# One change to a Fourier filter, expert layer and gated layer kernel: the first batch's transform rebuilt, and the weights converted at other places

## The chip, the cores and the metric

The kernel runs on one core of a Trainium2 chip. The metric is the device time of one execution, in microseconds (us); below, the median of three runs of the kernel before stands beside the one execution that was profiled.

## The reference

Three layers in a row, all in float32. `x` has 8 batches of 3072 positions of 256 features.

```python
X = np.fft.rfft(x, axis=1)                 # attn: a filter in the frequency domain
y = np.fft.irfft(X * (filt_r + 1j * filt_i)[None], n=3072, axis=1)
x1 = np.maximum(np.maximum(y @ w1, y @ w2), y @ w3) @ w_out      # 256 -> 768 -> 256
x_prev = shift_by_one_position(x1)         # zeros for the first position
xk, xr = mu_k * x1 + (1 - mu_k) * x_prev, mu_r * x1 + (1 - mu_r) * x_prev
k = np.maximum(xk @ w_k, 0)                # 256 -> 1024
out = sigmoid(xr @ w_r) * (k * k @ w_v)    # 1024 -> 256
```

[...]

## The kernel before, in words

A batch's transform of length 3072 is split into a transform of length 256 over one index (a matmul), a multiplication with twiddle factors, a transform of length 12 over the other index, the filter, and the same way back. Batches 1 to 7 do the transform of length 12 with VectorE's additions (`fft_all`, spread in small steps over the matmuls of the layers by a meter that counts costs; the order that comes out is fixed when the program is built). The first batch has nothing to hide behind, so `fft0` does it with matmuls and a trip through scratch memory in DRAM, ahead of everything else:

1. **Stage 1**, six units u. `load_x` brings a quarter of a unit of `x` in each of four transfers (`fetch_x`). `split_x` makes `xH` (VectorE cast) and `xL` (GpSimd subtraction). `stage1` is 12 matmuls into the PSUM tiles `re` and `im`. `twiddle` makes products `t` on ScalarE and sums `at` on VectorE, and writes `at` to the scratch `a0` in four transfers, two issued by SyncE (SP) and two by ScalarE (ACT). `clear_pad` zeroes rows 32 to 63 of nine tiles on ScalarE, since the two halves of the rows sit at partitions 0 and 64.
2. **The chunk loop**, eight chunks c of 1024 columns, two iterations each. `load_a` reads a chunk of the scratch into `rt`, `load_f` the filter into `ft` (four transfers), `spread_f` copies `ft` to its second half on ScalarE. An iteration is a matmul to `x0`, two VectorE products `zr` and `zi` with the filter, two matmuls back to `pv` (two iterations later), a ScalarE copy to `vo`, and per chunk two transfers of `vo` to the scratch `v0`. Chunk 0 alone needs extra matrices and extra filter rows (`special_f`, and a few bytes more behind `spread_f`).
3. Between these iterations, the generator `w1gen` converts w1, w2 and w3, 12 parts of 384 columns in two steps each. `W_STEPS` says how many steps go after each piece of `fft0`; in the loop it is two.

Then `load_v` brings the first tile back from `v0`, `untwiddle` and `stage_b` end the inverse transform, w_out is converted (`load_wo`), and the tiles t of the first layer begin: 48 tiles, each six `fblock`s (18 matmuls, two VectorE maxima `hm`, a split to `hH` and `hL`) and one `x1_out`. Between the first tiles' matmuls stand the first units of batch 1's transform (`load_x`, `fold` to `xe`, `dft_rows`).

Each engine runs its own instructions strictly in the order of the program, waits included. A transfer is issued by an engine's queue in the same order. SP issues nearly all of them.

Of the kernel before, what the change touches and what calls it, by code (L numbers as in the profile page):

```python
# [38 lines left out]
def own_tables():  # L39
# [35 lines left out]
    def spread(blocks, off, rows):  # L75
        n = 2 * M2
        o = np.zeros((off + n * len(blocks), 3, off + n * len(blocks)))
        for e, mats in enumerate(blocks):
            for i, m in enumerate(mats):
                for a in range(2):  # L80
                    for b in range(2):
                        part = m[a * M2:(a + 1) * M2, b * M2:(b + 1) * M2]
                        part = np.kron(part, np.eye(NH)) if rows else np.kron(np.eye(NH), part)
                        o[off * a + n * e:off * a + n * e + n, i, off * b + n * e:off * b + n * e + n] = part
        return o

    here, first = (fwd, inv, turned), (fwd0, inv0, turned0)
    named = {"m12": spread((here, here), 64, True), "m12s": spread((first, here), 64, True), "mside": spread((first,), 32, False)}
    named |= {"dft": rows(m), "up": rows(m + P), "idft": idft, "tw": tw}
# [3 lines left out]
def tile_fourier_moe_rwkv(ctx, tc, xl, fl, f0, dft24m, dft, idft, tw, w1, w2, w3, wo, muk, mur, wk, wv, wr, out):  # L93
# [5 lines left out]
    R1 = 4 * M2  # L99
    R2 = 64 + R1  # L100
# [3 lines left out]
    a0 = dram.tile([2, 2, RS, KC, P], F32, name="a0", tag="a0")  # L104
    v0 = dram.tile([2, 2, RS, KC, P], F32, name="v0", tag="v0")
# [75 lines left out]
    def from_f64(pool, tags, hi, lo, st, n):  # L181
        def tmp(dt, k):
            tag, bufs = tags[k]
            return pool.tile([P, n], dt, tag=tag, bufs=bufs, name=f"wt{k}")
# [8 lines left out]
        v, sg, r = tmp(I32, 1), tmp(I32, 2), tmp(I32, 1)  # L193
        u1, u2 = tmp(F32, 1), tmp(I32, 2)
# [6 lines left out]
        rf = tmp(F32, 2)  # L201
        scaled(rf, r, 2.0 ** -35)
        yield
        hb, pw = tmp(I32, 3), tmp(I32, 2)
# [61 lines left out]
    def fetch_x(xt, b, u):  # L266
        lower = xl[b // 2, :, :, u, b % 2].rearrange("h n (o x) -> o n h x", o=2)
        upper = xr[b // 2][:, 2 * u + b % 2].rearrange("h n (o x) -> o n h x", o=2)
        for k in range(2):
            for odd in range(2):  # L270
                if k == 0:
                    rows = lower[odd, :64]
                elif b:
                    rows = upper[1 - odd]
                else:
                    rows = lower[odd, 64:]
# [43 lines left out]
    def fft_all():  # L320
# [40 lines left out]
        load_f(0)  # L361
# [9 lines left out]
        for b in range(1, B):  # L371
            A = fp.tile([P, NH, M2, 2, P], F32, tag="A", name="A")
            for u in range(NU):
# [3 lines left out]
                if b == 1 and u < NH:  # L377
                    mirror_x(1, u)
                yield STOP
# [51 lines left out]
    AB = 4  # L431
    FBUF = 3
    LAG = 2
    ZB = 3
    mat_sb = pp.tile([R2, 3, R2], F32, name="mat_sb")
    mats_sb = pp.tile([R2, 3, R2], F32, name="mats_sb")
    upH = pp.tile([P, 2, P], F32R, name="upH")
    upL = pp.tile([P, 2, P], F32R, name="upL")

    def fft0():  # L440
        xt_t, xs_t, ps_t = {}, {}, {}

        rts = [m1.tile([R2, CH0], F32, tag=tag, name="rt", bufs=bufs) for tag, bufs in (("vt", 2), ("vt", 2), ("xo", 1))]
        fts = [pp.tile([R2, 2, CH0], F32, tag=f"f{i}", name="ft") for i in range(FBUF)]
        pads = [t[32:64] for t in rts] + [t[32:64, k] for t in fts for k in range(2)]

        def clear_pad():
            if pads:
                nc.scalar.mul(out=pads.pop(0), in_=tw_sb[32:64, 0, 0:1].to_broadcast([32, CH0]), mul=0.0)

        def load_x(u):
            xt_t[u] = pp.tile([P, 2, 512], F32, tag="a", name="xt", bufs=AB)
            fetch_x(xt_t[u], 0, u)

        def split_x(u):
            xt = xt_t.pop(u)
            xH = pp.tile([P, 2, 512], F32R, tag="b", name="xH", bufs=2)
            xL = pp.tile([P, 2, 512], F32R, tag="c", name="xL", bufs=2)
# [5 lines left out]
        def stage1(u):  # L464
            xH, xL = xs_t.pop(u)
            ps_t[u] = [bank([P, NH, 2, P], name) for name in ("re", "im")]
            for k, o in enumerate(ps_t[u]):
                of = o.rearrange("p h q c -> p (h q c)")
                mm3(of, dftH[:, k], dftL[:, k], xH[:, 0], xL[:, 0], True, False)
                mm3(of, upH[:, k], upL[:, k], xH[:, 1], xL[:, 1], False, True)  # L470

        def twiddle(u):
# [21 lines left out]
        rows_f = f0.rearrange("(k e h) r (kh x) -> e kh k h r x", e=2, h=NH, kh=2)  # L494

        def fetch_f(c):
            cs = slice(c * CH0, (c + 1) * CH0)
            for kh in range(2):
                for h in range(NH):
                    nc.sync.dma_start(out=fts[c % FBUF][RS * kh + h:RS * (kh + 1):NH], in_=rows_f[0, kh, :, h, :, cs])  # L500


        def special_f(t, at):
            for h in range(NH):
                nc.sync.dma_start(out=at(t, h), in_=rows_f[1, 0, 0:6, h, :, 0:P])

        def load_f(c):
            fetch_f(c)
            if c == 0:
                special_f(fts[0], lambda t, h: t[12 + h:24:NH, :, 0:P])  # L510

        def spread_f(c, k):
            nc.scalar.copy(out=fts[c % FBUF][64:R2, k], in_=fts[c % FBUF][0:R1, k])
            if c == 0:
                nc.sync.dma_start(out=fts[0][64:66, k, 0:P], in_=rows_f[0, 0, 6, :, k, 0:P])

        def load_a(c):
            for r in range(2):
                nc.sync.dma_start(out=rts[c % 3][64 * r:64 * r + R1], in_=af[r * R1:(r + 1) * R1, c * CH0:(c + 1) * CH0])

# [572 lines left out]
```

## Time and profile before

| | |
|---|---|
| median of 3 runs | 3218.6 us (3214.14 to 3220.53) |
| the profiled execution | 3208.55 us, its span on the core 3206.8 us |
| TensorE (PE) busy in the span | 3085.1 us (96%) |
| VectorE (DVE) | 2142.3 us (67%) |
| ScalarE (ACT) | 1474.6 us (46%) |
| GpSimd (POOL) | 1340.1 us (42%) |
| mean granted TensorE clock | 0.986 |

PE is busy almost throughout; only the first twentieth of the span shows it much below that. Times in rows are counted from the start of the span.

### The profile page before, as it was taken

Reading aid. Unit: us, or ns where it says so; the run is one execution under the profiler, and the core shown is the slowest. Engines: PE = TensorE matmul, PEld = TensorE weight load, DVE = VectorE, ACT = ScalarE, POOL = GpSimd, SP = SyncE. Lnnn points to the kernel's source line nnn. Section 1 sums busy time; section 2 is a strip of 40 time slices with the busy share of each in tenths; the row PEclk is TensorE's granted clock in tenths of the full one; section 3 lists DMA queues with packets and bytes.
Section 4 is the critical chain, followed back from the end, with each engine's and each line's share of the span. In section 5 each row is a group of like instructions: output and inputs, shape, how many; then the busy total and the mean of one; then the engine's idle time right before and its main releaser. Section 6 shows DMA issues by size and latency. Waiting matters only on the chain. (4 is left out here: it accounts for less than half of the span.)

```text
span 3206.8 us, 43665 instructions
## 1 busy us (share of the span) xinstructions
PE 3085.1 (96%) x16596; PEld 2629.2 (82%) x16596; DVE 2142.3 (67%) x2825; ACT 1474.6 (46%) x2744; POOL 1340.1 (42%) x988
## 2 busy tenths in 40 slices
PE   4689999999999999999999999999999999999999
PEld 2368787888888888887888888988899988898998
DVE  3749879589498597796794733555655555565555
ACT  3643343433433433434333534555555555555554
POOL 2273453633634634535333433444444344444343
PEclk7989999999999999999999999999999999999999
DMA  5632212212322112122111211111111111111110
GB/s 149 189 114 66 86 66 106 86 47 76 107 88 80 53 66 93 41 84 88 47 47 47 86 34 43 53 53 56 54 50 50 53 50 54 59 50 50 50 53 34
DMA packets 110743, 221.37 MB, mean 69 GB/s; under 512 B 11477, under 2 KB 51773, under 8 KB 108733
## 3 DMA queue, kind: packets, MB, share of 16 engines
q1 hardware_dynamic: 106244, 213.86, 20.0%
q10 hardware_dynamic: 4288, 4.72, 0.6%
q8 instruction: 130, 2.13, 0.3%
q14 instruction: 81, 0.66, 0.1%
HBM read 139.55 MB, written 90.00 MB: 72 GB/s over the span
## 5 line engine op out<-in xcount | busy, mean ns | idle before, releaser
L127 POOL TENSOR_TENSOR hL<-hm,hH 128x512 fp32r<-128x512 f32 x288 | 435.2, 1511 | 864.3 <-ACT hH L739 862.5
L127 DVE TENSOR_TENSOR hm<-p,hm 128x512 f32<-128x512 f32 x576 | 394.8, 686 | 345.5 <-PE p L124 290.1
L124 PE MATMUL pv<-wvh,kl 128*128 128x256 f32 x1536 | 431.0, 281 | 8.2 <-POOL kl L127 5.8
L127 POOL TENSOR_TENSOR ml<-tm,mh 128x512 fp32r<-128x512 f32 x192 | 249.2, 1298 | 451.7 <-ACT mh L828 451.7
L122 PE MATMUL pv<-wvh,kh 128*128 128x256 f32 x1536 | 426.3, 278 | 0.0
L123 PE MATMUL pv<-wvl,kh 128*128 128x256 f32 x1536 | 426.1, 277 | 0.0
L127 POOL TENSOR_TENSOR kl<-sq,kh 128x512 fp32r<-128x512 f32 x192 | 248.9, 1296 | 267.7 <-ACT kh L852 121.4
L731 ACT COPY hm<-p 128x512 f32<-128x512 f32 x288 | 168.4, 586 | 415.2 <-PE p L124 409.9
L828 ACT CAST mh<-tm 128x512 fp32r<-128x512 f32 x192 | 119.2, 621 | 490.7 <-DVE tm L130 490.7
L123 PE MATMUL pk<-ml,wkh 128*128 128x512 f32 x768 | 304.9, 397 | 0.2 <-POOL ml L127 0.2
L124 PEld LDWEIGHTS pv<-wvh,kl 128*128 128x128 f32 x1536 | 288.3, 188 | 18.0 <-POOL kl L127 18.0
L122 PE MATMUL pk<-mh,wkh 128*128 128x512 f32 x768 | 299.8, 390 | 0.0
L124 PE MATMUL pk<-mh,wkl 128*128 128x512 f32 x768 | 299.4, 390 | 0.0
L122 PEld LDWEIGHTS pv<-wvh,kh 128*128 128x128 f32 x1536 | 290.1, 189 | 0.0
L130 DVE SCALAR_TENSOR_TENSOR sq<-pk,rl 128x512 f32<-128x512 f32 x384 | 249.8, 680 | 57.9 <-ACT rl L847 57.9
L123 PEld LDWEIGHTS pv<-wvl,kh 128*128 128x128 f32 x1536 | 288.3, 188 | 0.0
L130 DVE SCALAR_TENSOR_TENSOR tm<-xt,mu_sb,tm 128x512 f32<-128x512 f32 x192 | 194.4, 1013 | 131.6 <-ACT tm L139 131.6
L739 ACT CAST hH<-hm 128x512 fp32r<-128x512 f32 x288 | 179.5, 623 | 221.1 <-DVE hm L127 220.7
L127 DVE TENSOR_TENSOR ot<-pv,sg 128x512 f32<-128x512 f32 x96 | 66.4, 692 | 298.0 <-issue 222.5
L127 DVE TENSOR_TENSOR kl<-sq,kh 128x512 fp32r<-128x512 f32 x192 | 221.6, 1154 | 31.9 <-ACT kh L852 15.7
L852 ACT ACTIVATE kh<-rl 128x512 fp32r<-128x512 f32 x384 | 240.8, 641 | 0.0
L847 ACT ACTIVATE rl<-pk 128x512 f32<-128x512 f32 x384 | 226.8, 603 | 4.4 <-DMA x1s<-xo 2.3
(163 smaller groups left out, 8073.0 us busy)
## 6 DMA issues: line engine op xcount, KB each, us to landing
xt<-x1s SPq DMA_DIRECT2D x40, 768.0 KB
x1s<-xo SPq DMA_DIRECT2D x96, 256.0 KB
out_dram<-ot SPq DMA_DIRECT2D x96, 256.0 KB
F<-in_fl_dram SPq DMA_DIRECT2D x14, 1536.0 KB
vs<-T SPq DMA_DIRECT2D x14, 1536.0 KB
vt<-vs SPq DMA_DIRECT2D x42, 512.0 KB
xt<-in_xl_dram SPq DMA_DIRECT2D x108, 128.0 KB
xt<-xr SPq DMA_DIRECT2D x84, 128.0 KB
```

The costliest lines, as they stand in the source:

```text
L122: nc.tensor.matmul(o, lh, rh, start=first, stop=False)
L123: nc.tensor.matmul(o, lh, rl, start=False, stop=False)
L124: nc.tensor.matmul(o, ll, rh, start=False, stop=last)
L127: (eng or nc.vector).tensor_tensor(out=o, in0=a, in1=b, op=op)
L130: nc.vector.scalar_tensor_tensor(out=o, in0=a, scalar=s, in1=b, op0=op0, op1=op1)
L731: nc.scalar.copy(out=hm, in_=ps[0])
L739: nc.scalar.copy(out=hH, in_=hm)
L828: nc.scalar.copy(out=hi, in_=tf)
L847: nc.scalar.activation(out=rl, in_=ps, func=AF.Relu)
L852: nc.scalar.activation(out=kh, in_=rl, func=AF.Square)
```

## The change

`x` comes in six transfers of 512 KB, one per unit, all in flight from the start (six buffers), with even and odd positions side by side. The matrices of stage 1 come as one table (`dft0`). The scratch `a0` and `v0` is laid out so that a chunk's rows are contiguous: `rt` and `vo` have 96 rows without a hole, one transfer instead of two; `at` is written by two transfers per unit, both on SP. Only the six halves of the `ft` tiles are still cleared, one in each unit. The chunks run in the order 1, 2, 3, 0, 4 to 7, and the filter of the first two chunks is loaded within stage 1. The small filter rows of chunk 0 are issued by ScalarE, the side filter `fs_sb` in the second tile, batch 1's filter later. Of the conversions, 8 parts stay in `fft0` (four steps between stage 1 and the loop, then one per iteration); the second halves of w2 and w3 and all of w_out (8 parts of 384 columns) move into the first tile (`load_late`, three steps after each fblock).

```diff
+        def load_x(u):
+            xt_t[u] = pp.tile([P, NH, 2, 256], F32, tag="a", name="xt", bufs=NU)
+            nc.sync.dma_start(out=xt_t[u].rearrange("p h o x -> p h (o x)"), in_=xl[0, :, :, u, 0].rearrange("h n x -> n h x"))
...
-            rows = a0.rearrange("r kh s k c -> kh k r s c")
+            rows = a0.rearrange("r s kh k c -> r (kh k) s c")
             for ri in range(2):
-                for kh in range(2):
-                    (nc.sync if kh else nc.scalar).dma_start(
-                        out=rows[kh, :, ri, 4 * u:4 * u + 4],
-                        in_=at[KC * kh:KC * (kh + 1), ri].rearrange("p q h c -> p (q h) c"))
+                nc.sync.dma_start(out=rows[ri, :, 4 * u:4 * u + 4], in_=at[:, ri].rearrange("p q h c -> p (q h) c"))
...
+        order = [1, 2, 3, 0] + list(range(4, NC))
...
         for u in range(NU):
-            if u == 4:
...
             stage1(u)
-            if u + AB - 1 < NU:
-                load_x(u + AB - 1)
-            for _ in range(2):
-                clear_pad()
-            if u == 3:
-                load_f(0)
             if u + 1 < NU:
                 split_x(u + 1)
+            nc.scalar.mul(out=pads[u], in_=tw_sb[32:64, 0, 0:1].to_broadcast([32, CH0]), mul=0.0)
             if u:
                 twiddle(u - 1)
+            if u in (1, 3):
+                load_f(order[u // 2])
             yield
...
+    def load_late():
...
+        parts = [(w_sb[("w2", "w3")[i // 2]], i % 2, st[:, i]) for i in range(4)]
+        parts = [(h[:, k, 384:], l[:, k, 384:], p) for (h, l), k, p in parts]
+        parts += [(hf[:, c:c + 384], lf[:, c:c + 384], so[:, c:c + 384]) for c in range(0, FB1 * D, 384)]
+        before = None
+        for i, (hi, lo, src) in enumerate(parts):
+            gen = from_f64(None, None, hi, lo, src, 384, lt[:, i % 2])
+            next(gen)
+            yield
+            if before:
+                next(before, None)
+                yield
+            before = gen
+        next(before, None)
...
-        W_STEPS = [0] * 5 + [1, 0] + [2] * 40
+        W_STEPS = [0] * NU + [4] + [1] * 40
...
         load_v(0)
-        wogen = load_wo()
-        next(wogen)
+        lategen = load_late()
+        next(lategen)
+        load_v(1)
+        fftgen = fft_all()
+        next(fftgen)
...
             for f in range(FB1):
                 fblock(t, f, step)
+                if t == 0:
+                    run_later()
+                    for _ in range(3):
+                        next(lategen, None)
```

On ScalarE in stage 1, the order before, from the products of unit 0 (t out of `im` and `re`) on; the rows named DMA are the writes of `at` to the scratch that ScalarE itself issues:

```order
L139 ACTIVATE t_210<-im,tw_sb 128x256 [waits PE_49]
L139 ACTIVATE t_211<-re,tw_sb 128x256
L139 ACTIVATE t_214<-im,tw_sb 128x256
L139 ACTIVATE t_215<-re,tw_sb 128x256
L490 DMA a_57<-at 64x4x128 [waits DMAHW7_49,DVE_49]
L490 DMA a_57<-at 64x4x128 [waits DMAHW1_49,DVE_49]
L449 ACTIVATE ft<-tw_sb 32x1024 x2
L139 ACTIVATE t_254<-im,tw_sb 128x256 [waits PE_49,Activation_49]
```

The same place of the change:

```order
L152 ACTIVATE t_205<-im,tw_sb 128x256 [waits PE_49]
L152 ACTIVATE t_206<-re,tw_sb 128x256
L152 ACTIVATE t_209<-im,tw_sb 128x256
L152 ACTIVATE t_210<-re,tw_sb 128x256
L556 ACTIVATE ft<-tw_sb 32x1024
L152 ACTIVATE t_245<-im,tw_sb 128x256 [waits DVE_49,PE_49]
```

The two writes, which wait for VectorE, have left ScalarE's order, and one zeroing stands between the units instead of two.

On SP around the end of stage 1 before, with the side filter, the last writes of `at`, three weight loads, the reads of the scratch and the filter loads of the second chunk:

```order
L505 DMA fs_sb<-in_f_dram 6x2x128 [waits DMAHW2_49]
L490 DMA a_57<-at 64x4x128 [waits DMAHW3_49,DVE_49]
L490 DMA a_57<-at 64x4x128 [waits DVE_49]
L490 DMA a_57<-at 64x4x128 [waits DMAHW5_49,DVE_49]
L490 DMA a_57<-at 64x4x128 [waits DMAHW6_49,DVE_49]
L178 DMA wst<-in_moe_w_dram 128x768
L178 DMA wst<-in_moe_w_dram 128x768 [waits DMAHW0_49]
L178 DMA wst<-in_moe_w_dram 128x768 [waits DMAHW1_49]
L490 DMA a_57<-at 64x4x128 [waits DMAHW2_49,DVE_49]
L490 DMA a_57<-at 64x4x128 [waits DMAHW3_49,DVE_49]
L519 DMA rt<-a_57 48x1024 [waits DMAHW5_49,DMAHW4_49,DMAHW2_49]
L519 DMA rt<-a_57 48x1024 [waits DMAHW6_49,DMAHW3_49]
```

The same place of the change:

```order
L521 DMA ft<-in_f_dram 12x2x1024 [waits DMAHW1_49]
L509 DMA a_57<-at 128x4x128 [waits DMAHW2_49,DVE_49]
L509 DMA a_57<-at 128x4x128 [waits DMAHW3_49,DVE_49]
L509 DMA a_57<-at 128x4x128 [waits DMAHW4_49,DVE_49]
L509 DMA a_57<-at 128x4x128 [waits DMAHW5_49,DVE_49]
L509 DMA a_57<-at 128x4x128 [waits DMAHW6_49,DVE_49]
L509 DMA a_57<-at 128x4x128 [waits DMAHW7_49,DVE_49]
L191 DMA wst<-in_moe_w_dram 128x768 [waits DMAHW0_49]
L191 DMA wst<-in_moe_w_dram 128x768 [waits DMAHW1_49,DVE_49]
L191 DMA wst<-in_moe_w_dram 128x768 [waits DMAHW2_49,DVE_49]
L540 DMA rt<-a_57 96x1024 [waits DMAHW6_49,DMAHW5_49,DMAHW7_49,DMAHW4_49,DMAHW3_49]
```

The side filter's loads are gone from this place, the first chunks' filter is ahead of the last writes instead of behind the reads of the scratch, and three weight loads, two of which wait for VectorE, stand between the last write and the first read.

On VectorE in the first tile of the change, from the last of `stage_b` through the first two fblocks (`hm` are an fblock's maxima, `lt` a late conversion):

```order
L140 TENSOR_TENSOR yL<-y_824,yH 128x512
L140 TENSOR_TENSOR hm<-p_856,hm 128x512
L140 TENSOR_TENSOR hm<-p_857,hm 128x512
L205 TENSOR_SCALAR lt<-wlst 128x384
L203 TENSOR_SCALAR lt<-wlst 128x384
L205 TENSOR_SCALAR lt<-wlst 128x384
L143 SCALAR_TENSOR_TENSOR lt<-wlst,lt 128x384
L205 TENSOR_SCALAR lt<-wlst 128x384
L203 TENSOR_SCALAR lt<-wlst 128x384
L205 TENSOR_SCALAR lt<-wlst 128x384
L143 SCALAR_TENSOR_TENSOR lt<-wlst,lt 128x384
```

Before, the three conversions of w_out (18 operations of 512 columns) stood at this place as one block ahead of the first `hm`; now eight parts stand in pieces behind each fblock's two maxima.

## Rows read from the trace of the kernel before

**Rows 1.** The profile's page, part 1: busy time, share, instructions

```profile
PE 3085.1 (96%) x16596; PEld 2629.2 (82%) x16596; DVE 2142.3 (67%) x2825; ACT 1474.6 (46%) x2744; POOL 1340.1 (42%) x988
```

**Rows 2.** Windows by stage: stretch, length, busy time of each engine, clock, DMA share, GB/s

```profile
0.00:46.04 46.04, 24.56 (x72) 16.05 (x72) 17.38 (x38) 20.46 (x36) 16.36 (x20) 0.86 0.55 143
46.04:72.31 26.27, 4.42 (x8) 1.98 (x8) 0.00 (x1) 3.75 (x5) 0.00 (x0) 0.56 0.68 162
72.31:133.46 61.15, 44.05 (x94) 16.49 (x94) 55.21 (x105) 46.95 (x77) 12.20 (x12) 0.96 0.61 168
133.46:149.74 16.28, 5.72 (x24) 5.15 (x25) 1.89 (x5) 3.52 (x7) 2.54 (x2) 0.58 0.71 203
149.74:213.34 63.60, 50.96 (x198) 38.73 (x197) 31.24 (x54) 31.96 (x61) 39.71 (x32) 0.87 0.50 161
213.34:3206.80 2993.46, 2955.41 (x16204) 2550.85 (x16202) 2036.61 (x2624) 1367.96 (x2558) 1269.29 (x923) 1.00 0.18 62
```

**Rows 3.** Timeline, one unit of stage 1: start, duration, engine, line, operation

```profile
25.34 1.54 ACTq L490 DMA_DIRECT2D a<-at  x2
...
26.11 2.62 POOL L127 TENSOR_TENSOR xL<-xt,xH 128x512 fp32r<-128x512 f32 x2 [3.51 <-DVE xH L460]
...
26.93 2.00 ACT L449 ACTIVATE ft<-tw_sb 32x1024 f32<-32x1024 f32 x2 [2.92 <-DVE xH L460]
...
30.56 0.48 DVE L130 SCALAR_TENSOR_TENSOR at<-re,tw_sb,t 128x256 f32<-128x256 f32 x1 [4.19 <-ACT t L139]
...
31.86 1.26 ACTq L490 DMA_DIRECT2D a<-at  x2
```

**Rows 4.** Timeline, first matmul of stage 1's units 0, 1 and 2

```profile
6.18 0.77 PE L122 MATMUL re<-xH,dftH 128*128 128x512 f32 x1 [6.18 <-DVE xH L460]
...
12.65 0.48 PE L122 MATMUL re<-xH,dftH 128*128 128x512 f32 x1
...
15.53 0.39 PE L122 MATMUL re<-xH,dftH 128*128 128x512 f32 x1
```

**Rows 5.** Timeline, from the last write of the scratch to the loop's first product

```profile
55.20 1.28 SPq L490 DMA_DIRECT2D a<-at  x2
60.16 2.67 SPq L519 DMA_DIRECT2D rt<-a  x6
62.88 6.79 SPq L500 DMA_DIRECT2D ft<-in_f_dram  x8
...
64.20 0.74 PE L586 MATMUL x<-rt,mats_sb 112*112 112x128 f32 x2 [25.08 <-DMA rt<-a]
...
72.31 0.69 DVE L127 TENSOR_TENSOR zr<-x,ft 112x512 f32<-112x512 f32 x1 [26.27 <-DMA ft<-in_f_dram]
```

**Rows 6.** Windows, a stretch of stage 1 with the transfers near their limit

```profile
27.00:30.00 3.00, 2.18 (x8) 1.52 (x9) 0.00 (x0) 2.97 (x5) 1.73 (x2) 1.00 0.99 261
```

**Rows 7.** Timeline, one iteration of the chunk loop on VectorE and one on ScalarE

```profile
94.29 0.68 DVE L127 TENSOR_TENSOR zr<-x,ft 112x512 f32<-112x512 f32 x1
...
98.64 0.68 DVE L127 TENSOR_TENSOR zr<-x,ft 112x512 f32<-112x512 f32 x1
...
96.33 1.04 ACT L513 COPY ft<-ft 48x1024 f32<-48x1024 f32 x1 [0.86 <-ACT vo L567]
97.40 0.51 ACT L206 CAST w2h<-wt 128x384 fp32r<-128x384 f32 x1
...
99.40 0.57 ACT L567 COPY vo<-pv 112x512 f32<-112x512 f32 x1
99.99 1.05 ACT L513 COPY ft<-ft 48x1024 f32<-48x1024 f32 x1
```

**Rows 8.** Timeline, SP reads the first tile back; and batch 1's first matmul

```profile
136.16 2.63 SPq L673 DMA_DIRECT2D vt<-v  x4
...
168.99 0.79 PE L122 MATMUL re<-xH,dftH 128*128 128x512 f32 x1 [4.50 <-ACT xH L339]
```

**Rows 9.** Windows, the stretch in which batch 1's transform runs on VectorE

```profile
230.00:377.00 147.00, 142.74 (x656) 118.33 (x656) 143.28 (x174) 49.27 (x94) 58.35 (x36) 0.98 0.18 62
```

More of the change, by code (lines that the diff above doesn't have):

```diff
@@ L440, in fft0 @@
     def fft0():
         xt_t, xs_t, ps_t = {}, {}, {}
-        rts = [m1.tile([R2, CH0], F32, tag=tag, name="rt", bufs=bufs) for tag, bufs in (("vt", 2), ("vt", 2), ("xo", 1))]
+        rts = [m1.tile([RT, CH0], F32, tag=tag, name="rt", bufs=bufs) for tag, bufs in (("vt", 2), ("vt", 2), ("xo", 1))]
         fts = [pp.tile([R2, 2, CH0], F32, tag=f"f{i}", name="ft") for i in range(FBUF)]
[L445 to L449, printed above, removed]
@@ L496, in fetch_f, with load_f @@
-        def fetch_f(c):
+                nc.sync.dma_start(out=rows[ri, :, 4 * u:4 * u + 4], in_=at[:, ri].rearrange("p q h c -> p (q h) c"))
+        def load_f(c):
             cs = slice(c * CH0, (c + 1) * CH0)
             for kh in range(2):
+                first = kh == 0 and c == 0
                 for h in range(NH):
[L500 to L505, printed above, removed]
@@ L512, in spread_f @@
         def spread_f(c, k):
-            nc.scalar.copy(out=fts[c % FBUF][64:R2, k], in_=fts[c % FBUF][0:R1, k])
+            nc.scalar.copy(out=ft_t[c][64:R2, k], in_=ft_t[c][0:R1, k])
             if c == 0:
[L515 to L519, printed above, removed]
+                nc.scalar.dma_start(out=ft_t[0][64:66, k, 0:P], in_=rows_f[0, 0, 6, :, k, 0:P])
@@ L531, in fft0, with load_a, pieces @@
+        af = a0.rearrange("r s kh k c -> (r s kh) (k c)")
+        vf = v0.rearrange("r s kh k c -> (r s kh) (k c)")
+        z_t, vo_t = {}, {}
+        def load_a(c):
+            nc.sync.dma_start(out=rt_t[c], in_=af[:, c * CH0:(c + 1) * CH0])
+        def pieces(c, j):
+            return ((1, slice(0, P)), (0, slice(P, 512))) if c == 0 and j == 0 else ((0, slice(0, 512)),)
+        for u in range(NU):
             load_x(u)
+            if u == 2:
+                yield
         yield
+        pads = [t[32:64, k] for t in fts for k in range(2)]
@@ L583, in fft0 @@
+        for i in range(3):
+            load_a(order[i])
+        load_f(order[2])
+        for k in range(2):
+            spread_f(order[0], k)
+        jobs = [(c, j) for c in order for j in range(SC)]
+        for i in range(len(jobs) + LAG):
+            if i < len(jobs):
+                c, j = jobs[i]
                 js = slice(j * 512, (j + 1) * 512)
                 x0 = bank([R2, 512], "x0")
-                for m, cs in pieces(i):
-                    nc.tensor.matmul(x0[:, cs], m[:, 0], rts[c % 3][:, js][:, cs], start=True, stop=True)
+                for m, cs in pieces(c, j):
+                    nc.tensor.matmul(x0[:, cs], m_sb[:RT, m, 0], rt_t[c][:, js][:, cs], start=True, stop=True)
@@ new lines, in fft0 @@
+            if i < len(jobs):
+                z = pp.tile([R2, 2, 512], F32, tag="a", name="z", bufs=NU)
+                zr, zi = z[:, 0], z[:, 1]
+                tt(zr, x0, ft_t[c][:, 0, js], mult)
+                tt(zi, x0, ft_t[c][:, 1, js], mult)
+                z_t[c, j] = (zr, zi)
+                k = i // SC
+                if j == SC - 1:
+                    if k + 3 < NC:
+                        load_a(order[k + 3])
+                    if k + FBUF < NC:
+                        load_f(order[k + FBUF])
+                if k + 1 < NC and j < 2:
+                    spread_f(order[k + 1], j)
```

229 lines of the change are left out of this document (108 added, 121 removed).

## The prediction, made before the changed kernel was run

> **What bounds the kernel now.** I read the page first. PE is busy 96% of the span [rows 1], so a gain has to come from a stretch in which PE stands. The windows by stage [rows 2] find it: from 213.34 us on PE is busy 2955.41 of 2993.46 us, 98.7%, and of the 213.34 us ahead of that, which end with the first tile, it is busy 129.7. The change touches only this part. I cut it into five stages: stage 1 to the last sum `at` (46.04 us), the handover to the loop's first product (26.27), the chunk loop to the issue of its last write (61.15), the way to the first fblock (16.28), and the first tile (63.60). Each has another limit.
>
> In stage 1 no engine is full: PE 24.56 us, ACT 20.46, DVE 17.38 of 46.04 [rows 2]. The timeline of one unit shows why [rows 3]. The reader is to follow one ring: ACT issues the writes of `at` at 25.34, which had to wait for DVE; behind them in ACT's order stand two zeroings (26.93, 2.00 us), then the products, and only then DVE makes the next `at` (30.56); ACT issues the next pair at 31.86. A unit takes 6.52 us, although POOL needs 2.62 for it [rows 3] and PE at its higher clock 2.88, from 12.65 to 15.53 [rows 4].
>
> In the handover DVE does nothing at all [rows 2]. The last write of the scratch is issued at 55.20, 9 us after its data was there, because SP's queue was behind; the reads follow at 60.16, PE at 64.20, and DVE waits until 72.31 for the last small filter rows, which SP issues only after eight loads for two later chunks (62.88 to 69.67) [rows 5].
>
> The loop is bound by DVE: 55.21 of 61.15 us [rows 2], 4.35 us from one `zr` to the next [rows 7].
>
> **The change, stage by stage.**
>
> *Stage 1.* The first matmul starts at 6.18 before. Now a table of 256 KB and one x of 512 KB must land, against 512 KB before, but with two issues instead of six; I keep 6.2. The first unit at the low clock takes 6.47 us, 6.18 to 12.65 [rows 4]; both halves of `xL` are needed for its second matmul, so I add 0.7: unit 0 ends at 13.4. The ring is cut, since ACT no longer issues writes; what is left per unit is PE 2.88, POOL 2.62, ACT 2.6 (one zeroing of 1.0, and 1.6 for four products, 28.93 to 30.56 [rows 3]), DVE at most 17.38/6 = 2.9 [rows 2]. PE and DVE are the longest; I take 3.1 for the handing over of buffers. Five more units end at 28.9, the last products and sums add 3.1: **32 us**. Lower bound 30 (2.88 each and no wait). Upper bound by the transfers: until the last write 8.6 MB must move (x 3.1, scratch 3.1, weights 1.2, filter 0.8, tables 0.6), and a stretch near its limit moved 261 GB/s at a share of 0.99 [rows 6]: 33 us after 2 us of start, and up to 38 if the 512-byte rows of the scratch hold them up. I stay near PE's figure, since the last write belongs to the next term.
>
> *Handover.* The filter's late rows and the side filter are out of the way: the first chunk is now chunk 1, whose filter is loaded in stage 1. From the last write's issue to PE it took 9.0 us (55.20 to 64.20) [rows 5]. Against that, SP now has three weight loads between, two of which wait for conversions on DVE; these fit into the 5 us in which SP waits for the writes to land anyway, but their 1.2 MB lie ahead of the reads, 4.4 us at 261 GB/s, partly hidden: 10.5. The first matmul at the low clock and the product's start add 1.5: **12 us**, bounds 9 and 17. The four conversion steps moved here cost nothing, as DVE has no other work until the data lands; without that cover they would cost about 6.
>
> *Loop.* Per iteration DVE keeps two products (1.2 to 1.4) and half a conversion; a conversion takes 4.35 less the products, about 3.0, so DVE falls to 2.8. PE needs 44.05/16 = 2.75. ACT becomes the longest: a whole iteration of it lasted 3.66 (96.33 to 99.99), of which 2.0 (97.40 to 99.40) was one conversion, and 0.86 was idle behind the writes of a chunk [rows 7]. A chunk (two iterations) now has one conversion: 2 x 1.66 + 2.0 + 0.9 = 6.2. The 12 conversion steps left cover six chunks: 37. Two chunks without run at PE's 5.5: 11. The two last inverse matmuls add 3. Chunk 0, with eight filter loads and five tables queued on SP in front of the next chunk, may make ACT wait some 2 us. **53 us**, bounds 47 (PE all through: 16 x 2.75 + 3) and 62 (nothing gained). Transfers do not forbid it: about 8.8 MB in 53 us is 166 GB/s, and the loop before moved 168 [rows 2].
>
> *Way to the first fblock.* Four reads of the scratch (2.63 us of issue [rows 8]) become two: 16.28 less 1 is **15.3**, bounds 14 and 17.
>
> *First tile.* Eight late conversions at 3.0 are 24 us of DVE; what leaves is w_out's block, by columns 3 x 512/384 x 3.0 = 12. DVE's 31.24 us of 63.60 [rows 2] become 43; POOL's 39.71 gain about 4 (1.0 for each late part); both still fit. PE in this tile is held by something else: batch 1's first matmul starts at 168.99, after 4.50 us of waiting [rows 8], and what it waits for is x, which comes behind w_out and the mirrored copy on SP. 1.5 MB of weights now come ahead of it, 1.5 MB of batch 1's filter goes behind it: even. But `dft_rows` of units 0 and 1 now stand together in PE's order, ahead of the fourth fblock, and POOL's 5 us for unit 1 lies open in part. I take **+2**, 65.6; bounds 60 and 80.
>
> *The rest* keeps its 2993.46: the order of its matmuls is the same. DVE is full from 230 to 377 (143.28 of 147), but PE is too (142.74) [rows 9], and the added conversions are over by then.
>
> **The sum**: 32 + 12 + 53 + 15.3 + 65.6 = 177.9 against 213.34, a gain of 35.4. The profiled execution would come from 3208.55 to 3173. The median of the runs lies 10 above it, and I predict the median: 3218.6 - 35.4 = **3183 us**.
>
> **A rule weighed against the trace.** [Rows 3] price the issue of a unit's two writes on ACT at 1.54 us, but the ring which they close at 6.52. The Trainium skill, DMA: Bandwidth & Descriptors, "Issuing engines are not separate DMA queues", says that issuing from several engines saves only the sequencer's time to start a transfer. By that rule taking the writes off ACT returns 6 x 1.54 = 9 us of ACT and loads SP with as much; stage 1 would come to about 37 instead of 32. I go by the rows, because what stands behind an issue that waits in an engine's order waits too.
>
> **The rivals.**
>
> *The loop is not freed* (0.14). A chunk's filter is issued when the chunk three before it is done (four issues of 6.79/8 = 0.85 [rows 5]), lands some 4 us later (60.16 to 64.20 for the reads) and must then be copied by ACT within about one and a half chunks. If that chain, not ACT's own work, sets the pace, a chunk takes 7.5, the loop 63, and the gain is 25; 3194. For it: ACT already waited behind writes [rows 7]. Against it: at 8.7 us a chunk no wait of DVE for a filter shows between these rows.
>
> *The first tile pays* (0.13). If the late conversions lie open (DVE's extra 12 and POOL's 4, since maxima and splits queue behind them and PE soon lacks banks), the tile takes 79 and the gain is 22; 3197. For it: PE waits in this tile in [rows 8]. Against it: DVE has half of the tile free [rows 2].
>
> *More than the sum* (0.08). The handover at 10, the loop at PE's pace of 47, the first tile unchanged: a gain of 46; 3173.
>
> *The other side, by PE's clock* (0.05). The handover before ran at a mean granted clock of 0.56, the loop at 0.96 [rows 2]. If PE stays at its low level of 1.2 GHz throughout, a unit of stage 1 takes 6.47 and each iteration 5.5: stage 1 ends at 48, the first product is at 60, the loop lasts 91, the last stages 81; 232, so 19 us slower, 3237. With stage 1 as forecast, it decides from 5.5 us an iteration on, where the loop takes 88 and the sum reaches 213. Against it: PE's share in the loop grows. The skill's page TensorE: Matmul & The Clock Gate, Part 1, names the same two levels and ties them to how busy PE was; the rows agree, as the low means stand where PE waited.
>
> **Chances and range.** The sum as worked out, with its terms each some microseconds off (gain 27 to 44, so 3175 to 3192): 0.60. The four rivals: 0.14, 0.13, 0.08, 0.05. The range goes from the case of more, 3169, to a first tile or loop that pays a little more than worked out, 3202; the case of the clock and the outer edges stay outside. A difference of 0.2% (6.4 us) is about what can be told from none: faster than that 0.93, within it 0.03, slower 0.04.
>
> **What would show it.** In the changed profile: units of stage 1 about 3.1 us apart on PE, the last `at` near 32; the first `zr` near 44; iterations of about 3.1 us with ACT the busiest; the first tile's read issued near 100; its last write of `x1s` near 178. Wrong it would be if `zr` waits for the filter in each chunk, if ACT waits for a filter copy, if the granted clock in the loop is near 0.5, or if the fourth fblock of the first tile stands far behind batch 1's second unit.

## The result, and the profile after

The changed kernel takes 3183.27 us (median of 4 runs, 3182.46 to 3185.88), the one before 3219.57 in the same comparison: a ratio of 0.9892, with an interval of 0.9875 to 0.9909. The forecast was 3183. A second comparison, on another chip, gave 3182.29 against 3212.58, 0.9901 [0.9884, 0.9918]. So the change saves 30 to 36 us by the medians. The two profiled executions differ by less, 3208.55 against 3184.06, and the stages below show why the agreement with 3183 is partly chance.

The page of the kernel after, part 1, answers to [rows 1]:

```profile
PE 3082.7 (97%) x16596; PEld 2633.6 (83%) x16596; DVE 2137.9 (67%) x2831; ACT 1472.8 (46%) x2745; POOL 1339.0 (42%) x989
```

The windows of the kernel after, cut at the same events as [rows 2] (last `at`, first product of the loop, issue of its last write, first fblock, write of the first `x1s`); columns: stretch, length, busy time of PE, weight loads, DVE, ACT, POOL, clock, DMA share, GB/s:

```profile
0.00:32.16 32.16, 21.05 (x72) 15.11 (x72) 14.96 (x38) 17.55 (x32) 16.61 (x20) 0.98 0.83 259
32.16:43.92 11.76, 2.11 (x3) 1.06 (x4) 5.75 (x15) 8.17 (x13) 1.00 (x1) 0.50 0.95 265
43.92:93.00 49.08, 45.99 (x100) 17.74 (x99) 33.53 (x68) 34.83 (x54) 7.03 (x7) 0.89 0.60 165
93.00:108.85 15.85, 6.02 (x25) 5.44 (x25) 2.19 (x5) 3.52 (x7) 2.55 (x2) 0.59 0.78 259
108.85:184.61 75.76, 50.49 (x197) 38.42 (x197) 46.00 (x84) 40.98 (x81) 44.63 (x37) 0.79 0.38 125
184.61:3182.20 2997.59, 2957.06 (x16204) 2555.86 (x16202) 2035.52 (x2624) 1367.74 (x2558) 1267.15 (x923) 1.00 0.18 63
```

Put beside the terms of the prediction:

| stage | before | forecast | after |
|---|---|---|---|
| stage 1 | 46.04 | 32 | 32.16 |
| handover | 26.27 | 12 | 11.76 |
| chunk loop | 61.15 | 53 | 49.08 |
| way to the first fblock | 16.28 | 15.3 | 15.85 |
| first tile | 63.60 | 65.6 | 75.76 |
| sum to the first tile's `x1s` | 213.34 | 177.9 | 184.61 |
| rest | 2993.46 | 2993.46 | 2997.59 |

Four terms hold to within 0.6 us, or came out better. The first tile lost 12.2 us where 2 were forecast, and is the step to be explained.

**Stage 1.** One unit in the timeline of the kernel after, which answers to [rows 3]; first the engines, then SP:

```profile
21.22 0.48 DVE L143 SCALAR_TENSOR_TENSOR at<-re,tw_sb,t 128x256 f32<-128x256 f32 x1 [0.75 <-ACT t L152]
...
24.36 0.48 DVE L143 SCALAR_TENSOR_TENSOR at<-re,tw_sb,t 128x256 f32<-128x256 f32 x1 [0.79 <-ACT t L152]
...
21.21 1.06 ACT L556 ACTIVATE ft<-tw_sb 32x1024 f32<-32x1024 f32 x1
22.75 0.47 ACT L152 ACTIVATE t<-im,tw_sb 128x256 f32<-128x256 f32 x1 [0.48 <-PE im L137]
...
21.08 2.40 SPq L509 DMA_DIRECT2D a<-at  x4
```

A unit's first sums stand 3.14 us apart here (21.22 to 24.36). ACT now waits for PE (`im`) and for nothing of DVE's: the ring through ACT's writes is gone. PE is the longest: the 2.88 us of a unit [rows 4] and some 0.2 more, in which it waits for POOL's `xL` at the unit's second matmul.

**Handover.** SP, PE and DVE at the end of stage 1 (against [rows 5]):

```profile
35.51 1.27 SPq L540 DMA_DIRECT2D rt<-a  x3
...
41.81 4.58 PE L589 MATMUL x<-rt,m_sb 96*112 96x512 f32 x5 [12.94 <-DMA rt<-a]
...
43.92 1.29 DVE L140 TENSOR_TENSOR z<-x,ft 112x512 f32<-112x512 f32 x2 [5.88 <-PE x L589]
```

DVE's first product now waits for PE and no longer for filter rows. (In the second profile of the changed kernel, at the end of the experiments, its wait of 5.95 us is put down to a load of the filter again, at nearly the same time, 44.38.) What remains is the way of the data: 6.3 us from the issue of the reads to PE, in a stretch that moved 265 GB/s at a DMA share of 0.95, near the 261 of [rows 6]. So its length may now be set by the bytes it moves; no run tried that.

**Loop.** A conversion makes the two float32r halves, `hi` and `lo`, of 384 columns of a float64 weight; in the trace it is six operations of DVE, four of ACT and, for `lo`, one of POOL. PE, then DVE, SP and ACT, in the kernel after (against [rows 7]):

```profile
64.27 1.18 PE L589 MATMUL x<-rt,m_sb 96*112 96x512 f32 x2 [1.95 <-DMA rt<-a]
...
78.44 1.02 PE L589 MATMUL x<-rt,m_sb 96*112 96x512 f32 x2
...
81.02 1.02 PE L589 MATMUL x<-rt,m_sb 96*112 96x512 f32 x2
...
63.51 0.69 DVE L140 TENSOR_TENSOR z<-x,ft 112x512 f32<-112x512 f32 x1 [3.26 <-DMA ft<-in_f_dram]
65.62 0.69 DVE L140 TENSOR_TENSOR z<-x,ft 112x512 f32<-112x512 f32 x1 [1.42 <-DMA ft<-in_f_dram]
...
70.40 0.42 DVE L140 TENSOR_TENSOR dftL<-stage,dftH 128x256 fp32r<-128x256 f32 x1 [1.96 <-ACT dftH L916]
...
53.95 0.36 SPq L911 DMA_DIRECT2D stage<-table_dft  x1
...
76.56 1.04 ACT L526 COPY ft<-ft 48x1024 f32<-48x1024 f32 x1 [0.38 <-ACT vo L573]
...
82.25 1.04 ACT L526 COPY ft<-ft 48x1024 f32<-48x1024 f32 x1 [0.38 <-ACT vo L573]
```

The iterations stand 2.58 us apart on PE, with half a conversion in them or without. ACT takes 5.69 us for a chunk with a conversion (76.56 to 82.25), more than PE's 5.16 for two iterations, but PE does not wait for it: its waits in the loop are 1.95 us for a read and 0.5 for DVE. Three iterations in the middle of the loop, from 59.6 to 73.3, take 4.69, 5.20 and 3.81, some 6 us lost, where DVE waits for filters and for the split of a table, and PE for that read, of the scratch (at 64.27): what SP issues behind the tables is late. The granted clock of the loop is 0.89, not near 0.5, so the rival by PE's clock fell.

**First tile.** What PE waited for in it, by the view of waits (engine, line, released by: sum, times, longest), before and after:

```profile
PE re L122 <- ACT xH L339: 6.2, 2, 4.5
PE im L122 <- ACT xH L339: 0.7, 1, 0.7
```

```profile
PE re L135 <- ACT xH L349: 13.5, 2, 7.9
PE im L135 <- ACT xH L349: 7.0, 1, 7.0
```

With the waits for `xL`, 4.3 us before and 4.6 after, the sum was about 11 us and is 25: PE waits longer for the operands of batch 1's units, and its mean granted clock in the tile fell from 0.87 [rows 2] to 0.79. DVE, POOL and ACT in the tile's first 30 us:

```profile
132.84 0.36 DVE L203 TENSOR_SCALAR lt<-wlst 128x384 int32<-128x384 int32 x1 [8.68 <-POOL w2l L140]
...
125.65 2.48 POOL L140 TENSOR_TENSOR xe<-xt 128x512 f32<-128x512 f32 x2 [4.97 <-DMA xt<-xr]
...
131.80 1.00 POOL L140 TENSOR_TENSOR w2l<-lt 128x384 fp32r<-128x384 f32 x1
...
134.09 0.52 ACT L152 ACTIVATE lt<-lt 128x384 f32<-128x384 int32 x1 [1.64 <-DVE lt L143]
...
139.18 0.62 ACT L349 CAST xH<-xe 128x512 fp32r<-128x512 f32 x1
```

This reads like one chain: POOL waits for x, the end of a late conversion (`w2l`) stands behind that on POOL, DVE's next conversion waits 8.68 us for its temporaries, and ACT's cast for unit 1 stands behind ACT's part of that conversion. It was my first theory, and the experiments tested it against three others: that x lands late behind the added weights on SP; that units 0 and 1 now stand together on PE; and that it is simply the amount of late work, wherever it waits.

### The profile page after: what moved, and what is told of

Its sections match the earlier page's. It is cut to its first block, busy times and chain, and to the rows that moved or that the text cites. A ratio compares the mean times of both kernels' runs of the same rounds, so it can differ in the third digit from the quotient of the medians.

```text
span 3182.2 us, 43568 instructions
## 1 busy us (share of the span) xinstructions
PE 3082.7 (97%) x16596; PEld 2633.6 (83%) x16596; DVE 2137.9 (67%) x2831; ACT 1472.8 (46%) x2745; POOL 1339.0 (42%) x989
## 3 DMA queue, kind: packets, MB, share of 16 engines
q10 hardware_dynamic: 904, 3.15, 0.3%
## 5 line engine op out<-in xcount | busy, mean ns | idle before, releaser
L143 DVE SCALAR_TENSOR_TENSOR tm<-xt,mu_sb,tm 128x512 f32<-128x512 f32 x192 | 194.7, 1014 | 131.6 <-ACT tm L152 131.6
```

The lines of the kernel that those rows point to most:

```text
L143: nc.vector.scalar_tensor_tensor(out=o, in0=a, scalar=s, in1=b, op0=op0, op1=op1)
```

## The experiments

Each edit is made to the changed kernel. "First tile" is the time from the first fblock's matmul to the write of the first `x1s`, 75.76 above. The comparisons ran on several chips, each with the kernel before beside it; so ratios are compared, and microseconds of the whole kernel only with care.

**Where the two profiles of before and after differ from their medians.** The kernel before, once more.

> The kernel before, unchanged, profiled once more. Its profiled execution took 3208.55 us, 10 us below its median of 3219.57, while that of the changed kernel (3184.06) agrees with its median. If the first profile was a lucky one, this one takes 3217 to 3221 with the first 213 us as in rows 2 and the 10 us spread over the rest; if the median carries something that a profile does not, it takes 3208 to 3210 again.

It took 3216.93. The write of the first `x1s` is issued at 214.92 against 213.34, the last of the `x1s` writes at 1989.86 against 1984.81, and what follows is 3.25 us longer: 1.6 of the 8.4 us lie in the part that was changed, the rest is spread over the same instructions later on. The first profile was a short one. By the first `x1s`, before and after stand 28.7 us apart in the first pair of profiles and 28.2 in the second (214.92 against 186.75 in the run of the changed kernel at the end of this section).

**The writes of `at` on ACT again.**

```diff
-                nc.sync.dma_start(out=rows[ri, :, 4 * u:4 * u + 4], ...)
+                nc.scalar.dma_start(out=rows[ri, :, 4 * u:4 * u + 4], ...)
```

> The changed kernel, but with the two writes of each `at` issued by ACT again. Ring theory: ACT's products, two sums on DVE, the issue that waits for them (1.5), one zeroing (1.0) and the next products (1.6) stand in a circle of about 5.1 us, so a unit takes 5.1 instead of 3.07, the last `at` comes at 42 instead of 32.2, and the time grows by 8 to 11 us. The rule that only the issue's own time counts: ACT per unit 2.6 + 1.5 = 4.1, the last `at` at 37, 5 us more. If stage 1 gained by its fewer loads of x and not by the ring: last `at` at 32 to 33, no difference.

3191.22, ratio 0.9924 [0.9906, 0.9942], 8 to 9 us above the medians of the changed kernel. Its window of stage 1, and two units on ACT and DVE:

```profile
0.00:40.66 40.66, 21.72 (x72) 15.40 (x72) 16.02 (x38) 17.52 (x32) 16.79 (x20) 0.90 0.69 214
```

```profile
21.51 0.93 ACTq L509 DMA_DIRECT2D a<-at  x2
22.49 1.05 ACT L556 ACTIVATE ft<-tw_sb 32x1024 f32<-32x1024 f32 x1 [2.30 <-DVE xH L480]
...
26.47 0.93 ACTq L509 DMA_DIRECT2D a<-at  x2
...
25.17 0.48 DVE L143 SCALAR_TENSOR_TENSOR at<-re,tw_sb,t 128x256 f32<-128x256 f32 x1 [2.62 <-ACT t L152]
30.12 0.48 DVE L143 SCALAR_TENSOR_TENSOR at<-re,tw_sb,t 128x256 f32<-128x256 f32 x1 [2.62 <-ACT t L152]
```

The ring is back, as the first case of the expectation had it: ACT's issue, zeroing, products, DVE's sums, ACT's issue, 4.95 us a round (25.17 to 30.12), and stage 1 is 8.5 us longer. ACT's busy time is the same (17.52 against 17.55), and the two issues take 0.93 us a unit, 5.6 in all. The rule of the Trainium skill that was weighed in the prediction (DMA: Bandwidth & Descriptors, "Issuing engines are not separate DMA queues") prices only that issue time. In this kernel the trace goes past it: the issue waits for DVE, and all of ACT's order waits with it.

**Chunk 0 first.**

```diff
-        order = [1, 2, 3, 0] + list(range(4, NC))
+        order = list(range(NC))
```

> The changed kernel with the chunks in their natural order, 0 first, so that the special filter rows are needed for the first product. Theory: what DVE waited 8 us for in the handover was small rows issued after eight loads for later chunks, not chunk 0 as such; with its eight filter loads issued in stage 1 the first product comes at 44 to 47, and the 4 to 6 us which DVE and ACT wait for chunk 0's filter in the middle of the loop are gone: -5 to +1 us in all. Rival, the order of the chunks is what freed the handover: first product at 50 to 53, 4 to 8 us slower.

3185.79, ratio 0.9910 [0.9894, 0.9926]. The first product is at 49.22, between the two cases, and the loop keeps its loss. What SP waited for between 20 and 46 us, SP's first reads of the scratch, and DVE in the handover and the loop:

```profile
SPq L191 <- DMA ft<-in_f_dram: 5.6, 1, 5.6
```

```profile
42.27 2.62 SPq L540 DMA_DIRECT2D rt<-a  x3
...
49.22 1.29 DVE L140 TENSOR_TENSOR z<-x,ft 112x512 f32<-112x512 f32 x2 [10.99 <-PE x L589]
...
72.54 0.42 DVE L140 TENSOR_TENSOR dftL<-stage,dftH 128x256 fp32r<-128x256 f32 x1 [5.26 <-ACT dftH L916]
```

So of the 14.5 us that the handover gained, the order of the chunks is worth 5.3 (in the other profiles whose edit leaves this stage alone it came between 42.45 and 45.11). It works through SP and not through the special rows: SP's weight loads, which stand ahead of the reads, wait 5.6 us for a filter load, the reads are issued at 42.27 instead of 35.51, and DVE waits for PE. The other 9 us go with the loads taken off SP ahead of the reads and with the fewer transfers of the scratch; no run parts these. And my reading of the loss in the loop was wrong: with chunk 0 out of its middle the iterations there still take 3.15, 7.08 and 4.00 us. DVE stands 5.26 us at the split of a table, behind ACT, whose filter copy waited 1.99 us for a load that SP issued after the five tables. Which of the two, the tables or the split, would free the loop alone was not tried.

**All twelve conversions in the loop, two steps an iteration.**

```diff
-        for c, names in ((0, (w1, w2, w3)), (384, (w1,))):
+        for c, names in ((0, (w1, w2, w3)), (384, (w1, w2, w3))):
-        W_STEPS = [0] * NU + [4] + [1] * 40
+        W_STEPS = [0] * NU + [4] + [2] * 40
```

(The names stand here for the pairs in the code; the late part keeps only `wo`.)

> The changed kernel with all 12 conversions of w1, w2, w3 in the chunk loop at two steps an iteration, so that only w_out's four parts are late. Theory: ten iterations become DVE's 4.35 us (rows 7) and the loop takes 58 to 63 instead of 49.1; the first tile gets 4 to 6 us of its 12 back; 4 to 8 us slower in all. Rival, the loop was freed by its transfers and not by DVE: the loop stays at 49 to 52 and the time falls by 3 to 6.

3186.98, ratio 0.9913 [0.9896, 0.9931]. The loop and the first tile:

```profile
44.23:105.98 61.75, 47.18 (x100) 16.75 (x99) 49.81 (x92) 43.57 (x70) 11.16 (x11) 0.92 0.60 156
122.02:188.36 66.34, 49.65 (x198) 38.11 (x197) 37.27 (x60) 32.80 (x65) 40.71 (x33) 0.82 0.39 127
```

With two steps an iteration DVE is the bound again, with iterations of 4.35 us as in [rows 7], and the loop is 12.7 us longer. So it is the lighter load on DVE that freed the loop, as forecast. The first tile, with four late conversions instead of eight, is 9.4 us shorter.

**Four ways to break the chain in the first tile.** The low parts of the late conversions on DVE:

```diff
-        tt(lo, rf, f32(pw), mult, nc.gpsimd)
+        tt(lo, rf, f32(pw), mult, nc.gpsimd if slots is None else None)
```

> The changed kernel with the last step of the eight late conversions (the low parts) on DVE instead of POOL, so that DVE's next conversion no longer waits for POOL, which stands behind the wait for x. Theory of the chain DVE behind POOL behind x: the 8.68 us wait of DVE is gone, first tile 66 to 70 instead of 74.9, 5 to 8 us faster. If the landing of x or the two units side by side set the tile: within 2 us of no change. If DVE's volume does: 8 x 0.5 to 0.8 = 4 to 6 us slower.

Batch 1's copy and x ahead of the late weights on SP:

```diff
+        fftgen = fft_all()
+        next(fftgen)
         lategen = load_late()
         next(lategen)
         load_v(1)
-        fftgen = fft_all()
-        next(fftgen)
```

> The changed kernel with batch 1's mirrored copy and first x loads issued on SP ahead of the late weights instead of behind them. Theory that x lands late because of the weights ahead: x lands 4 to 6 us earlier, PE's wait for unit 0 (5.54 us) goes, 4 to 6 us faster. Chain theory: DVE's wait for POOL shrinks by as much as x comes earlier, but the first conversions come later: -4 to +2. If neither: no change.

Units 0 and 1 apart:

```diff
                 yield STOP
+                if i == 0:
+                    yield STOP
                 sgen = split_x(i + 1)
```

> The changed kernel with one stop more in batch 1's transform, so that its units 0 and 1 stand apart on PE with the fourth fblock between them, as in the kernel before. Theory of the two units: POOL's and ACT's work for unit 1 lies behind the fblock, the wait of 7.93 us goes, 6 to 8 us faster. Chain theory: the fblock waits for `hm` and banks behind DVE's wait just as unit 1 did; 0 to 3 us faster.

The late steps dealt out otherwise:

```diff
-                    for _ in range(3):
+                    for _ in range((5, 4, 0, 3, 3, 3)[f]):
```

> The changed kernel with the late steps dealt out 5, 4, 0, 3, 3, 3 over the first tile's six fblocks instead of 3 each, so that no conversion stands in a queue behind the first wait for x. Chain theory: DVE's 8.68 us wait is gone at the price of about 2 us more in the first two fblocks, 4 to 7 us faster. If x or the two units set the tile: within 2 us. If it is the conversions' volume: within 2 us.

Ratios 0.9905 [0.9888, 0.9921], 0.9910 [0.9896, 0.9925], 0.9913 [0.9898, 0.9927] and 0.9911 [0.9896, 0.9926]: none can be told from the changed kernel. The first tile takes 76.98, 77.63, 79.30 and 77.40 us. In the four profiles whose edit leaves the tile alone (the changed kernel twice, the writes on ACT, chunk 0 first) it takes 75.76, 76.93, 76.00 and 77.15, so only the third is clearly longer, and none is shorter. The chain and the two units fall as single causes; for x the edit decides less, as shown below. In the first DVE's wait for POOL is gone, and another stands in its place, of nearly the same length:

```profile
133.20 0.88 DVE L143 SCALAR_TENSOR_TENSOR vp<-vt,tw_sb,b 128x256 f32<-128x256 f32 x2 [8.13 <-ACT b L152]
```

Without POOL's step ACT's casts for unit 0 still wait 7.50 us, until 126.80, for POOL's sums of x, its part of the conversions stands behind them, and DVE then waits for ACT.

In the second POOL begins with x 17.2 us after the first fblock (127.81 less 110.62), no earlier than before the edit (125.65 less 108.85 is 16.8), but for another reason. SP's issue of the reads of x that POOL's first sum needs, in the changed kernel:

```profile
121.98 1.23 SPq L287 DMA_DIRECT2D xt<-xr  x2
```

The same with the edit, and then DVE and POOL with the edit:

```profile
113.87 1.23 SPq L287 DMA_DIRECT2D xt<-xr  x2
...
122.80 0.36 DVE L205 TENSOR_SCALAR lt<-wlst 128x384 int32<-128x384 int32 x1 [6.53 <-DMA wlst<-in_moe_w_dram]
...
126.86 0.99 POOL L140 TENSOR_TENSOR w2l<-lt 128x384 fp32r<-128x384 f32 x1 [8.57 <-ACT w2h L221]
127.81 2.61 POOL L140 TENSOR_TENSOR xe<-xt 128x512 f32<-128x512 f32 x2
```

SP's reads of x go out 8 us earlier, and POOL no longer waits for x. But now the weights are late: DVE waits 6.53 us for them, and POOL's sums of x stand behind the late conversion. The edit exchanged one late load for the other; what the tile would take with both in time was not tried.

In the third the fourth fblock stands between the units and PE's 7.93 us for unit 1 fall to 1.79, but 7.99 us at unit 2 are still there, and the fblock itself now waits for its own late weights:

```profile
138.24 0.80 PE L135 MATMUL p<-yH,w3h 128*128 128x512 f32 x1 [3.02 <-ACT w3h L221]
```

In the fourth DVE's longest wait for POOL is 3.37 us, and PE's wait for unit 1 is 8.77.

**Fewer hops between DVE and ACT.** ACT's three operations within a late conversion done on DVE:

```diff
-        nc.scalar.activation(out=u1, in_=v, func=AF.Relu, scale=-1.0, bias=...)
-        nc.scalar.activation(out=u2, in_=u1, func=AF.Relu, scale=-1.0, bias=...)
+        ts(u1, v, -E_LO, add, 0.0, ALU.max)
+        ts(u2, u1, E_SPAN, ALU.min)
...
-        scaled(rf, r, 2.0 ** -35)
+        ts(rf, r, 2.0 ** -35, mult)
```

(shortened; for the late conversions alone)

> The changed kernel with three of the four ACT operations of each late conversion done on DVE (about 0.35 us each there, 8 x 3 x 0.35 = 8 us more DVE in the tile), so that ACT no longer waits for DVE in the middle of a conversion. Theory that the late work costs by its hops between DVE and ACT, which stand ahead of the casts of `xH` in ACT's order: first tile 66 to 71 instead of 75.8, 4 to 9 us faster. Theory that it costs by DVE's volume: 77 to 82, 2 to 6 us slower.

3183.84, ratio 0.9911 [0.9896, 0.9925]. Its first tile:

```profile
106.47:185.00 78.53, 51.23 (x197) 38.27 (x197) 62.71 (x108) 27.96 (x57) 46.08 (x37) 0.80 0.37 121
```

DVE has 16.7 us more, ACT 13.0 less, and the tile 2.8 more. The theory of the hops (66 to 71) falls. The tile lies in the range given for DVE's volume (77 to 82), but 16.7 us of DVE cost only 2.8, so DVE's time by itself does not set it either. Only 8 of the 16.7 were expected; the rest are operations that run slower beside POOL's (last section).

**All twelve in the loop, one step an iteration.** As above, with `W_STEPS` as in the changed kernel.

> The changed kernel with all 12 conversions of w1, w2 and w3 at one step an iteration of the chunk loop, what is left of them behind the first tile's inverse, and only w_out's four parts late. The iterations of the changed loop stand 2.58 us apart on PE with a half conversion or without; so if PE sets this loop up to one step an iteration, the loop stays at 49 to 51, and the first tile falls to 66 to 68 as with half the late conversions: 7 to 10 us faster than the changed kernel. If each conversion costs its 2.4 us wherever it is put: loop 55 to 60, no gain in all.

3175.42, ratio 0.9890 [0.9873, 0.9906]. Loop and first tile:

```profile
44.49:97.09 52.60, 48.26 (x100) 17.80 (x99) 40.61 (x87) 40.03 (x65) 8.99 (x9) 0.86 0.66 185
113.05:179.80 66.75, 48.74 (x197) 37.63 (x197) 35.07 (x64) 33.39 (x67) 42.35 (x35) 0.84 0.39 131
```

The tile is 9.0 us shorter, the loop 3.5 longer: its iterations keep 2.58 us, and the 3.5 lie in its last four, where a filter lands late (ACT waits 1.81 us at 87.08) and conversions stand between the last products. The write of the first `x1s` is issued at 179.80, 4.8 us earlier than in the changed kernel. By its ratio this version cannot be told from the changed kernel (0.9892, 0.9901).

**Two edits together.** The same, without steps in the loop's last four iterations, and with chunk 0 as the last chunk.

```diff
-        order = [1, 2, 3, 0] + list(range(4, NC))
+        order = list(range(1, NC)) + [0]
-        W_STEPS = [0] * NU + [4] + [1] * 40
+        W_STEPS = [0] * NU + [4] + [1] * 14 + [0] * 40
```

> All 12 conversions of w1, w2, w3 in the loop at one step an iteration, but none in its last four (the rest behind the first tile's inverse), and chunk 0 as the last of the eight instead of the fourth. Chunk 0 in the middle costs three iterations of 4.69, 5.20 and 3.81 us where the others take 2.58, so 6 us; if its eight filter loads then have time to land, the loop takes 43 to 46 instead of 49.1; if they don't, DVE waits for them at the end and it stays at 49 to 51. First tile 66 to 68. In all 9 to 15 us faster than the changed kernel by the profiles, 3169 to 3175.

3187.29, ratio 0.9918 [0.9903, 0.9933]; beside it on the same chip the changed kernel took 3182.29, so this is 5 us slower by the medians, where 9 to 15 us faster were expected. The loop takes 55.81 us and the tile 72.83. The loss in the middle of the loop stays (one iteration of 6.67 us, with DVE at the split of a table for 5.38), which fits the run with chunk 0 first; near the end DVE now waits four times more (0.82, 1.75, 1.96 and 2.10 us), for filter copies, a staged weight and a conversion. And the conversions that were held back stand ahead of the first fblock's maxima on DVE, so their cost is the tile's again.

**The changed kernel once more.**

> The changed kernel, unchanged, beside the one before and the combination on one chip. The medians of the kernel before differed by 11 us between chips, and its single runs by 16. If its first comparison holds, the ratio is 0.987 to 0.991 again and the profiled execution comes within 3 us of 3184; the first tile takes 75 to 77 us again.

3182.29, ratio 0.9901 [0.9884, 0.9918], profiled 3182.23; first tile 76.93. With the two runs that leave the tile alone (76.00, 77.15), one profile of this stage is good to about 1.4 us; the two profiles of the kernel before differ by 1.2 (63.60, 64.81).

## Why the number was right, and which step was not

**Right.** Stage 1: the ring set the pace and not a full engine; putting ACT's issues back brings 8.5 us of the 13.9 back; the other 5.4, one zeroing a unit among them, no run parts. Handover: with fewer loads ahead of the reads and the late filter rows gone it takes 11.76 of the forecast 12, and 5.3 of its gain is the chunks' order. Way to the first fblock: 15.85 against 15.3.

**Right in kind, off in size: the loop.** Forecast 53 with ACT setting the pace at 3.1 us an iteration, 6.2 a chunk; measured 49.08, with PE setting it at 2.58. ACT's sum was nearly right: 5.69 for a chunk with a conversion, the difference being the idle time behind the writes, 0.38 us and not 0.86. What failed is that ACT's sum would be the pace: it lags behind PE where a chunk has a conversion, and PE does not wait for it. The lower bound that the prediction named, PE all through at 47, was the better one. The rival that waits for filters hold up every chunk did not come about; they and the tables cost about 6 us at one place, where 2 were allowed for.

**The step that failed: the first tile.** The prediction took +2 for it, because "both still fit": DVE had half of the tile free. The added work was priced nearly right (DVE 43 forecast and 46.00 measured, POOL 4 more and 4.9), but the share of busy time of each engine was the wrong measure of the room for it. The table sets the tile's length beside the sum of the busy times of DVE, ACT and POOL, from the windows of each kernel. The last column is a straight line laid through the first and the third row, 63.60 + 0.424 x (sum - 102.9), so 0.42 us of tile for each us of the sum.

| kernel | DVE | ACT | POOL | sum | first tile | line |
|---|---|---|---|---|---|---|
| before | 31.24 | 31.96 | 39.71 | 102.9 | 63.60 | 63.6 |
| before, again | 31.32 | 32.04 | 39.65 | 103.0 | 64.81 | 63.6 |
| after | 46.00 | 40.98 | 44.63 | 131.6 | 75.76 | 75.8 |
| after, again | 46.32 | 40.96 | 44.64 | 131.9 | 76.93 | 75.9 |
| 12 in the loop, two steps | 37.27 | 32.80 | 40.71 | 110.8 | 66.34 | 66.9 |
| 12 in the loop, one step | 35.07 | 33.39 | 42.35 | 110.8 | 66.75 | 66.9 |
| two edits together | 45.59 | 38.04 | 44.95 | 128.6 | 72.83 | 74.5 |
| low parts on DVE | 55.78 | 40.71 | 37.40 | 133.9 | 76.98 | 76.7 |
| fewer hops | 62.71 | 27.96 | 46.08 | 136.8 | 78.53 | 77.9 |
| late steps dealt out | 46.97 | 41.10 | 44.77 | 132.8 | 77.40 | 76.3 |
| x first | 49.89 | 41.24 | 45.30 | 136.4 | 77.63 | 77.8 |
| units apart | 46.09 | 40.95 | 44.38 | 131.4 | 79.30 | 75.7 |

It holds within 1.7 us for all but the last, whose order on PE is another one. It is a summary and not a price: the runs that only move work change the sum by 5 us at most, which is 2 us of tile on this line and hardly more than the 1.4 between profiles of the same tile. What is shown: the loss goes with the number of late conversions, 2.3 us for each (9.0 to 9.4 for four), and moving their work between engines or in the order does not take it away. What is only argued is why: the three engines go through one program order, each operation needs one of another engine, and when one of them stands at the wait for x the others come to stand within a few us, so that what follows runs largely in turn and not side by side. The chain that I read first is one instance of it; with its link cut, the next queue waited as long, and with x in time the weights came late. Two parts stay open: what the late loads cost apart from the work, and what of the loss is DVE's slowing beside POOL, some 9 of its 46.00 us (last section). No run here left the late work out altogether.

**Why 3183 all the same.** By the first `x1s` the change gains 28 to 29 us and not 35.4: the loop's surplus of 4 does not make up for the tile's 10. The first comparison of medians gave 36.3, the second 30.3, while the rest of the kernel, with the same matmuls, takes from 2993 to 3000 us in the four profiles of the two kernels. So the hit on 3183 is in part luck: the median before in that comparison, 3219.57, is the highest of the five that were taken of this kernel. Against the second comparison the forecast gain is 5 us too large. The rival "the first tile pays" named 79 us for it and 22 us of gain; the truth lies between it and the sum.

**What a version would need.** Twelve conversions at one step an iteration looks like the better split: 6.9 us below the changed kernel by the medians of two comparisons, 4.8 to 7.0 by the first `x1s` (179.80 against 184.61 and 186.75). Against the kernel before, their ratios overlap, and the two were not timed on one chip, so that it beats the changed kernel is likely and not settled.

## What to carry to other kernels

An issue or any instruction that waits in an engine's order makes everything behind it wait: price the round that it closes, not its own time (0.93 us of issue cost 1.8 us a unit here). Where several engines work through one program order with operations that need each other, free time on one of them need not be room: ask what each operation waits for, and put extra work where a different engine sets the pace and leaves regular gaps, as PE did in the chunk loop at 2.58 us an iteration. Before a cause is read from one chain of waits, cut one link: here the wait came back elsewhere with 8.13 us in place of 8.68. And after an edit that brings a load forward, look at what it pushed back: x came 8 us earlier, and the weights were then waited for 6.53 us.

## What the runs showed of the hardware

The same DVE operation of a conversion takes about four times as long in places where POOL is at work. In the first tile of the kernel after, six of the conversions' TENSOR_SCALAR operations take 1.30 to 1.47 us, each beside one of POOL's; clear of POOL's they take 0.35 or 0.36. DVE twice, and POOL beside the second:

```profile
118.99 0.36 DVE L203 TENSOR_SCALAR lt<-lt 128x384 int32<-128x384 int32 x1
...
140.82 1.31 DVE L203 TENSOR_SCALAR lt<-lt 128x384 int32<-128x384 int32 x1
...
140.34 2.93 POOL L140 TENSOR_TENSOR xL<-xe,xH 128x512 fp32r<-128x512 f32 x2
```

So a conversion has no one price: its cost depends on what POOL does at that time. Over the tile's 48 operations of this kind (the SCALAR_TENSOR_TENSOR ones take 0.55 or 0.56 us when clear of POOL's), the time above the price of an undisturbed one adds up to about 9 us of DVE's 46.00; with ACT's operations moved to DVE, 72 operations, to about 18 of 62.71. And the kernel before had medians of 3208.87 to 3219.57 us in five comparisons, 0.3% apart, with nothing changed in the kernel.
